# An attention and gated-MLP block on one core: a new order for background sums, more staging rows, norm transposes by DMA, and merged half tiles

## The chip, the cores and the metric

The kernel runs on one core of one Trainium2 chip. The metric is the device time in microseconds of one execution. Before the change it was 876.59 us (median of three runs, 875.39 to 877.72). The kernel before had medians of 873.2 to 876.6 us in different sessions, 0.4% apart, so each experiment is compared with the runs of the kernel before of its own session, on the same chip.

## The reference

One transformer block with 2,048 tokens of width 640, 32 heads of width 20, and a gated MLP of width 1,728, all in bf16:

```python
x = A_x                                    # 1 x 2048 x 640
h = x + attention(layernorm(x), wqkv, wo)  # softmax(q k^T / sqrt(20)) v, 32 heads
n = layernorm(h)
out = h + ((n @ w_gate) * (n @ w_up)) @ w_down
```

The score matrix is the large thing: 32 heads x 2,048 x 2,048 exps.

## The kernel before

The program is one static schedule. A small planner in Python keeps a model of the engines, picks at each step what TensorE (PE) does next, and so fixes the order of every engine's instructions. The lines of all matmuls are one helper line, so in the profile the tile names tell them apart.

Queries come in six chunks of 512, 512, 384, 256, 256 and 128. For each chunk PE makes scores into PSUM tiles `A` (two tiles, of three and of two banks), ScalarE (ACT) takes the exp of a whole tile into `E`, and PE sums `E` with the values into the bank `acc`. Between these, PE does background sums: the projections of Q, K and V, and then the second stage of the chunk before (output projection `W`, LayerNorm, transposes, gate and up sums, down sums). All of these share only two PSUM banks, `m`, until attention has ended.

Some of the exps are made on VectorE (DVE) from integer arithmetic, to take load off ScalarE. Such a score bank goes into a free `m` bank if there is one. If there is none, and the tile `A` with three banks is next, its third bank is used instead; then ACT's instruction covers only two banks:

```python
ok = fr and self.flat < M_END                 # fr: the m banks that are free now
if ok or size == 3:
    mine = banks if ok else banks[:2]
    ...
    if pick is not None and ok:
        dbank = min(fr, key=lambda b: b.free.t)   # an m bank; ACT keeps its full tile
    elif pick is not None:
        third = Bank(A[u][:, 2, :])               # the third bank of A; ACT gets two
```

The choice of PE's next work (first number: the earliest time, then the rank; lower goes first):

```python
opts.append((max(ep, t), 0, pact))                # value sums
opts.append((max(eb, t), 1, self.bg_act(g)))      # background sums
opts.append((es, 2, sact))                        # scores
```

Heads beyond the first eight have their Q and K projected densely, 120 rows at a time, and unpacked through DRAM. DVE moves the finished sum from its `m` bank into one of two staging rows, a DMA writes that out, another reads it back in the wanted layout:

```python
stg = tiles(p1, 2, [P, QW], BF16, "stg")
...
r = en.add("DVE", dve_ns(w), [e, stg_free[k]], ... copy of ps into stg[k] ...)
e = dma(write, [r], size=TW * w * 2)
stg_free[k] = e                                   # free when the DMA has landed
```

The norm of the second stage is transposed by PE, 20 column-tiled matmuls against the identity for each 128 x 640 tile, and copied from PSUM by DVE into `ln2T`. The MLP width of 1,728 is 13 tiles of 128 and one of 64; gate and up are two sums of five steps for each.

The softmax here doesn't subtract the row's maximum and nothing guards it: scores larger than these inputs give would overflow.

## Time and profile before

| | before |
|---|---|
| median | 876.59 us |
| profiled span | 873.6 us |
| first exp starts | 17.0 us |
| exps on ACT, busy | 800.0 us in 749 instructions, 1,746 banks |
| ACT pauses between exps | 20.5 us |
| last exp to the end | 36.1 us |
| exps on DVE | 302 banks, 176 from `m` and 126 from `A` |

The four rows from the first exp on (17.0, 800.0, 20.5 and 36.1) add to the span; that sum is how I read this kernel throughout. "Pauses" is worked out: end of the last exp, less start of the first, less busy time. Busy tenths in 40 equal slices of the span, which show that PE, DVE and ACT are all full in the middle, and that ACT has little to do in the last two slices:

```profile
PE   6999999989999999999999999999999999999998
...
DVE  5654587989879999999989999989999999889562
ACT  4789999999999999999999999999999999998931
```

The other two rows that matter are the second half of the DVE exps, and the copies after the PE transposes (count, then busy us and mean ns, then idle time before):

```profile
L745 DVE TENSOR_SCALAR i<-A 128x512 int16<-128x512 f32 x126 | 86.5, 686 | 11.5 <-PE A L432 10.0
...
L1026 DVE COPY ln2T<-m 128x640 bf16<-128x640 bf16 x15 | 7.2, 483 | 0.2 <-PE m L1017 0.2
```

### The profile page before, as it was taken

To read this page: it belongs to the slowest core of one execution; us is meant where nothing else is said; L and a number is where in the kernel's file an instruction comes from. 1 tells how busy PE (TensorE), PEld (TensorE's weight loads), DVE (VectorE), ACT (ScalarE), POOL (GpSimd) and SP (SyncE) were. 2 spreads that over 40 slices of the span, in tenths; PEclk is the share of its full clock that TensorE was granted. 3 is DMA by queue.
4 is the path that set the end of the run, shared out by engine and by line. 5 is a ranking of instruction groups with operands and counts; after the bars stand their busy time and mean duration, and the time that the engine had idled before them with its cause. 6 is when DMAs were issued, how large, how long until landed. Compare 5 with 4: busy or idle time off the path is not lost.

```text
span 873.6 us, 35178 instructions
## 1 busy us (share of the span) xinstructions
PE 828.6 (95%) x15727; PEld 366.7 (42%) x15727; DVE 741.9 (85%) x1579; ACT 808.8 (93%) x771; POOL 21.3 (2%) x33
## 2 busy tenths in 40 slices
PE   6999999989999999999999999999999999999998
PEld 3344333223333322233444333344444444556676
DVE  5654587989879999999989999989999999889562
ACT  4789999999999999999999999999999999998931
POOL 3020000000000000000000000000000000000000
PEclk8899999999999999999999999999999999999999
DMA  7221221222221143320030223134024411164200
GB/s 209 64 58 49 79 67 31 78 76 67 69 79 29 28 105 103 78 63 18 30 91 13 57 66 81 27 84 105 17 51 94 96 32 32 32 150 86 52 6 24
DMA packets 131755, 56.23 MB, mean 64 GB/s; under 512 B 102292, under 2 KB 129556, under 8 KB 131604
## 3 DMA queue, kind: packets, MB, share of 16 engines
q1 hardware_dynamic: 131604, 53.99, 24.3%
q8 instruction: 123, 2.02, 1.0%
q14 instruction: 28, 0.23, 0.1%
HBM read 45.63 MB, written 8.09 MB: 61 GB/s over the span
## 4 chain that ended last, share of the span: by engine, by line
ACT 63%; PE 26%; DVE 6%; issue 5%; DMA 0%; DVEq 0%; POOL 0%; ACTq 0%
ACT E L731 62%; PE m L432 11%; PE A L432 6%; PE acc L432 5%; PE b L432 2%; DVE i L745 2%; DVE fr L775 1%; PE m L1017 1%; DVE ED L778 1%; DVE st L989 0%; DVE fr L769 0%; DVE hl L772 0%; DVE gs L1410 0%; DMA shared<-in_A_x_dram 0%; DVE shared L1001 0%
## 5 line engine op out<-in xcount | busy, mean ns | idle before, releaser
L731 ACT ACTIVATE E<-A 128x1536 bf16<-128x1536 f32 (+1 forms) x749 | 800.0, 1211 | 20.6 <-PE A L432 18.4
L432 PE MATMUL A<-qT,kT 32*128 32x256 bf16 (+3 forms) x3063 | 292.7, 298 | 24.1 <-ACT E L731 21.9
L432 PEld LDWEIGHTS <-kT 32*128 32x128 bf16 (+1 forms) x3448 | 100.1, 92 | 248.2 <-issue 215.0
L432 PE MATMUL acc<-E,Vx 128*32 128x256 bf16 (+3 forms) x2832 | 190.7, 304 | 4.8 <-ACT E L731 3.8
L745 DVE TENSOR_SCALAR i<-m 128x512 int16<-128x512 f32 x176 | 120.4, 685 | 13.5 <-PE m L432 12.5
L432 PEld LDWEIGHTS <-Vx 128*32 128x32 bf16 x3328 | 70.1, 95 | 100.5 <-issue 91.6
L775 DVE TENSOR_TENSOR fr<-hl,fr 128x1024 bf16<-128x1024 bf16 x151 | 103.4, 685 | 2.0
L778 DVE TENSOR_TENSOR ED<-i,fr 128x1024 int16<-128x1024 int16 x151 | 103.0, 682 | 1.3
L745 DVE TENSOR_SCALAR i<-A 128x512 int16<-128x512 f32 x126 | 86.5, 686 | 11.5 <-PE A L432 10.0
L432 PE MATMUL m<-Wd,hh 128*32 128x320 bf16 (+1 forms) x1498 | 79.9, 301 | 1.4 <-issue 0.9
L432 PE MATMUL m<-lnT,Wr 128*32 128x512 bf16 (+7 forms) x1200 | 74.7, 345 | 1.8 <-DVE lnT L1026 0.8
L432 PE MATMUL m<-ln2T,wu 128*32 128x512 bf16 (+2 forms) x980 | 69.5, 348 | 0.8 <-DVE i L745 0.4
L432 PE MATMUL m<-ln2T,wg 128*32 128x512 bf16 (+2 forms) x980 | 69.2, 349 | 0.3 <-DVE hh L1421 0.2
L432 PE MATMUL acc<-zt 128*32 128x512 bf16 (+3 forms) x1012 | 68.5, 346 | 0.0
L432 PE MATMUL m<-qT,kT 32*128 32x256 bf16 (+3 forms) x265 | 68.0, 310 | 0.0
L772 DVE TENSOR_SCALAR hl<-fr 128x1024 bf16<-128x1024 int16 x151 | 63.5, 421 | 1.5
L769 DVE TENSOR_SCALAR fr<-i 128x1024 int16<-128x1024 int16 x151 | 62.1, 417 | 0.7
L432 PEld LDWEIGHTS <-hh 128*32 128x32 bf16 (+2 forms) x1540 | 42.2, 96 | 28.1 <-issue 15.5
L1421 DVE TENSOR_TENSOR hh<-gs,m 128x512 bf16<-128x512 bf16 (+3 forms) x70 | 37.9, 541 | 14.0 <-PE m L432 10.1
L432 PE MATMUL m<-shared,On 128*32 128x320 bf16 x960 | 44.7, 300 | 0.7 <-DVE i L745 0.4
L432 PEld LDWEIGHTS <-Wr 128*32 128x32 bf16 (+1 forms) x1200 | 28.9, 97 | 27.0 <-issue 16.7
L1410 DVE CAST gs<-m 128x512 bf16<-128x512 f32 (+2 forms) x64 | 36.0, 562 | 4.7 <-PE m L432 4.3
(85 smaller groups left out, 542.7 us busy)
## 6 DMA issues: line engine op xcount, KB each, us to landing
wg<-in_B_w_gate_dram SPq DMA_DIRECT2D x47, 160.0 KB
wu<-in_B_w_up_dram SPq DMA_DIRECT2D x47, 160.0 KB
rb<-rd SPq DMA_DIRECT2D x16, 256.0 KB
kT<-kq SPq DMA_DIRECT2D x24, 128.0 KB
kq<-stg SPq DMA_DIRECT2D x24, 120.0 KB
out_dram<-ot SPq DMA_DIRECT2D x16, 160.0 KB
shared<-in_A_x_dram SPq DMA_DIRECT2D x14, 160.0 KB
Wd<-in_B_w_down_dram SPq DMA_DIRECT2D x13, 160.0 KB
```

Source lines behind the costliest of these rows:

```text
L432: nc.tensor.matmul(out_, lhsT=lhsT, rhs=rhs, start=start, stop=stop)
L731: apart(readers, nc.scalar.activation(E[:, 0:size, :], src[:, 0:size, :], ACT.Exp, scale=LN2_ / UNIT))
L745: apart(readers, nc.vector.tensor_scalar(it[:, pos, :], bank.ap, BIAS, 0.0, ALU.add, ALU.max))
L769: nc.vector.tensor_scalar(f[:, 0:n, :], it[:, 0:n, :], 127, None, ALU.bitwise_and)
L772: nc.vector.tensor_scalar(h[:, 0:n, :], f[:, 0:n, :], QR, QK, ALU.subtract, ALU.mult)
L775: nc.vector.tensor_tensor(fb[:, 0:n, :], h[:, 0:n, :], f[:, 0:n, :], ALU.mult)
L778: nc.vector.tensor_tensor(e16[:, 0:n, :], it[:, 0:n, :], fb[:, 0:n, :], ALU.add)
L1017: nc.tensor.transpose(pt[32 * i:32 * i + 32, c * P:(c + 1) * P], src[:, c * P + 32 * i:c * P + 32 * i + 32], ident[:])
L1410: r = en.add("DVE", dve_ns(w), [e, was], lambda: nc.vector.tensor_copy(gs[0:M, 0:w], ps[0:M, 0:w]), 1)
L1421: r = en.add("DVE", dve_ns(w), [e, ce, was], lambda: nc.vector.tensor_tensor(hh[0:M, 0:w], gs[0:M, 0:w], ps[0:M, 0:w], ALU.mult), 1)
```

## The change

There are four parts.

**Order**: a background sum that already has a bank goes ahead of value sums, while no more than 14 exp'd banks wait for their value sum. **Rows**: five staging rows in place of two; they lie inside `ln2T`, which nothing else uses that early. **DMA turn**: in the first four chunks the norm tiles are transposed by a DMA. **Halves**: the half gate and up tiles lie side by side in one 128-wide weight tile and are summed at once.

```diff
+BACK = 14
-            opts.append((max(eb, t), 1, self.bg_act(g)))
+            opts.append((max(eb, t), 1 if g.bank is None or len(self.att.E) > BACK else -1, self.bg_act(g)))
...
-    stg = tiles(p1, 2, [P, QW], BF16, "stg")
+    stg = [ln2T[:, i, :] for i in range(KC)]
...
+TURNP = 4
+    def turn_rows(src, dst, deps, prio):
+        return dma(lambda: nc.sync.dma_start_transpose(dst, src), deps, prio=prio, size=2 * P * D * 2)
...
+                if p < TURNP:
+                    lev[i] = turn_rows(l2[i % 2][:], ln2T[:, :, i * P:(i + 1) * P], [e, fr.get("ln2T")], 0.5)
+                    fr["ln", i % 2] = lev[i]
+                    continue
...
+                if M < P:
+                    ...   # ev_gu: cast ps[0:M] to gs[M:2M], then hh = gs[M:2M] * ps[M:2M]
+                    gg = sum_group(..., [(wg[:, c, :], ln2T[:, c, 0:w]) for c in range(KC)], w, P, ev_gu, f"g{p}{f}")
```

Left out of this diff are the weight loads that put both halves into one tile.

More of the change, by code (lines that the diff above doesn't have):

```diff
@@ L1296, in hold @@
         w_ = tile_ap.rearrange("p (c f) -> p c f", c=KC)
-        e = dma(lambda: nc.sync.dma_start(w_[:, :, 0:M], src), deps, size=n, prio=3)
+        at = M if which == 1 and M < P else 0
+        e = dma(lambda: nc.sync.dma_start(w_[:, :, at:at + M], src), deps, size=n, prio=3)
         p2["held"][which, f] = (w_, e)
@@ L1322, in prefetch @@
         for n in range(2 * (NF - RES)):
-            ap, e = spots[n]
+            ap, e = spots[min(n, 2 * (NF - RES) - 2)]
             hold(n % 2, RES + n // 2, ap, [e])
@@ L1399, in more @@
                     src, _, n = weight(1, f)
-                    eu = dma(lambda wu=wu, src=src, M=M: nc.sync.dma_start(wu[:, :, 0:M], src), [fr.get(("wu", k))], prio=2, size=n)
+                    if M < P:
+                        eu = dma(lambda wg=wg, src=src, M=M: nc.sync.dma_start(wg[:, :, M:2 * M], src), [fr.get(("wg", k))], prio=2, size=n)
+                    else:
+                        eu = dma(lambda wu=wu, src=src, M=M: nc.sync.dma_start(wu[:, :, 0:M], src), [fr.get(("wu", k))], prio=2, size=n)
                 gk = gsn[0] % 2
@@ L1403, in more, with ev_gu @@
                 gs = T["gs"][gk]
+                if M < P:
+                    cu = Cell()
+                    def ev_gu(ps, e, gs=gs, M=M, cu=cu, hh=T["hh"][f], was=fr.get(("gs", gk)), then=fr.get(("hh", f))):
+                        cast = lambda: (nc.scalar.copy if last else nc.vector.tensor_copy)(gs[M:2 * M, 0:w], ps[0:M, 0:w])
+                        r = en.add("ACT", w / 1.2 + 63.0, [e, was], cast, 1) if last else en.add("DVE", dve_ns(w), [e, was], cast, 1)
+                        cu.t2 = en.add("DVE", dve_ns(w), [r, then], lambda: nc.vector.tensor_tensor(
+                            hh[0:M, 0:w], gs[M:2 * M, 0:w], ps[M:2 * M, 0:w], ALU.mult), 1)
+                        return cu.t2
+                    fr["gs", gk] = cu
+                    gg = sum_group(list(lev.values()) + [eg, eu, fr.get(("hh", f))], [(wg[:, c, :], ln2T[:, c, 0:w]) for c in range(KC)], w, P, ev_gu, f"g{p}{f}")
+                    if not held:
+                        fr["wg", k] = gg.ev
+                    groups.append(gg)
+                    hhev.append(cu)
+                    ups.append(gg.ev)
+                    continue
                 ce = Cell()
```

## The prediction

> **What bounds the kernel now.** I read the page first: busy times, then the chain that ended last. After that the waits, then windows of the busy times by stage, and last the timeline of the two ends. The page:
>
> ```profile
> span 873.6 us, 35178 instructions
> PE 828.6 (95%) x15727; PEld 366.7 (42%) x15727; DVE 741.9 (85%) x1579; ACT 808.8 (93%) x771; POOL 21.3 (2%) x33
> ...
> ACT 63%; PE 26%; DVE 6%; issue 5%; DMA 0%; DVEq 0%; POOL 0%; ACTq 0%
> ...
> L731 ACT ACTIVATE E<-A 128x1536 bf16<-128x1536 f32 (+1 forms) x749 | 800.0, 1211 | 20.6 <-PE A L432 18.4
> ...
> L745 DVE TENSOR_SCALAR i<-m 128x512 int16<-128x512 f32 x176 | 120.4, 685 | 13.5 <-PE m L432 12.5
> ...
> L432 PE MATMUL acc<-zt 128*32 128x512 bf16 (+3 forms) x1012 | 68.5, 346 | 0.0
> ```
>
> PE is the busiest by its share, but it does not bind: the last row above, `acc<-zt`, multiplies a tile of zeros, filler put where PE has nothing to do (76.5 us with its smaller groups, summed over windows of that tile). What binds is the exp on ScalarE (L731): 749 instructions, 800.0 us busy, 63% of the chain. Over time (columns: stretch, length, busy of PE, PEld, DVE, ACT, POOL with counts, clock, DMA share, GB/s):
>
> ```profile
> 60.00:140.00 80.00, 77.60 (x1406) 31.79 (x1402) 51.58 (x106) 77.53 (x71) 0.00 (x0) 1.00 0.22 65
> 140.00:300.00 160.00, 151.46 (x2298) 54.71 (x2290) 137.58 (x280) 159.46 (x155) 2.07 (x2) 1.00 0.21 60
> 300.00:740.00 440.00, 423.14 (x8011) 176.12 (x8009) 424.68 (x861) 435.50 (x407) 4.08 (x5) 1.00 0.26 62
> 740.00:838.00 98.00, 95.64 (x2772) 58.38 (x2768) 75.19 (x176) 93.38 (x91) 0.70 (x1) 1.00 0.34 74
> ```
>
> From 60 to 740 us ACT is 97 to nearly 100% busy. The span is therefore a sum of four terms: 17.0 us before the first exp (timeline), 800.0 us of exps, 20.5 us of ACT pauses among them, and 36.1 us from the last exp (837.5) to the end at 873.6. Where the pauses lie, from the waits (us in total, times, longest):
>
> ```profile
> ACT gs L1408 <- PE b L432: 27.4, 10, 20.3
> ACT E L731 <- PE A L432: 18.4, 17, 3.5
> ```
>
> The first is the tail, in which ACT only copies gate sums. Of the second, 8.6 us lie between 16 and 60 us, 2.4 from 60 to 120, 2.9 from 300 to 520 and 3.0 after 780. In the tail the timeline shows PE working almost without a gap (838 to 870 us): the rest of the fifth query chunk's gate and up sums, its down sums, then the same for the sixth. So the tail is bound by PE work left over when attention ends.
>
> VectorE matters because it takes exps off ScalarE. L745 with its four followers does 302 (176 from `m`, shown above, and 126 from `A`) of the 2,048 score banks (the scheduler's cap is 17%, about 320), ScalarE the other 1,746. One bank on DVE costs 0.685 us plus half of the four two-bank rows (0.417 + 0.421 + 0.685 + 0.682 = 2.205, so 1.10): 1.79 us. On ACT one costs 800.0 / 1,746 = 0.46 us. DVE is 97% busy from 300 to 740 (424.68 of 440), but idle 28 us in 60 to 140 and 22 us in 140 to 300.
>
> **What the Trainium skill says.** "VectorE: DVE Perf Modes", The three transpose paths, puts a 128x128 bf16 transpose at 390 ns on TensorE into PSUM and at 1,309 ns by DMA into SBUF. The trace of before has only the PE path: 20 column-tiled instructions for a whole 128x640 tile take 0.46 us together, far below five times the page's figure; no run yet shows the DMA. "DMA: Bandwidth & Descriptors", DMA Transpose (X-bar), says that two transposing streams in flight at once can corrupt each other; here all DMAs come from one queue, so no new wait should follow. "TensorE: Matmul & The Clock Gate", Part 4, says the PE's output goes to PSUM and needs a copy: agreed, there are 16 such copies into ln2T at 0.48 us each. "TensorEngine Tiling (Array Packing)", Key Properties, says that tiles of the array run independently: agreed, four column-tiled matmuls of 512 columns that each last some 390 ns come out in a group of 0.39 us, so a 64-wide tile fills half of the array in the same time.
>
> **The change part by part.**
>
> Norm transposes by DMA, in the first four chunks (4 + 4 + 3 + 2 = 13 of 16 row tiles). Removed: 13 x 20 transposes, 13 x 0.46 = 6.0 us of PE, and 13 copies, 13 x 0.483 = 6.3 us of DVE (row L1026), and 13 holdings of one of the only two `m` banks. Added: 13 DMAs of 160 KB. My estimate for one: five blocks at the skill's 1.31 us are 6.5 us if nothing overlaps, about 3 us if it moves like other transfers (held weights of 160 KB ran at 222 GB/s near 785 us, 0.7 us each, plus receipt). The scheduler plans for 0.73 of issue, 2.05 of transfer and 3.5 of landing, 6.3 us. The DMA queues carry 24.3% of their capacity. The PE share is hidden wherever filler runs. The DVE share is not: 6.3 / 1.79 is 3.5 exps moved, 3.5 x 0.46 = **1.6 us less on ACT**.
>
> Half gate and up tile in one sum. The last tile is 64 wide. Two sums of five become one of five; the cast and the product on DVE stay. Saved PE: five steps over all the columns of each chunk. A sum of five over 128 columns starts every 0.28 us in the tail (timeline), 0.44 ns a column and step, so 5 x 2,048 x 0.44 = 4.5 us. Only what lies after about 640 us, where background work runs over into the tail, is worth time: chunks of 384, 256, 256 and 128 columns, 5 x 1,024 x 0.44 = 2.2 us. The transposes of the third and fourth chunks add 5 x 0.46 = 2.3 us. Filler after 640 us still takes about 7 us, so part of it is hidden. I take two thirds of 4.5: **3 us off the tail**.
>
> Five staging rows. The dense K/Q projections stage in two rows that are freed only when a DMA has landed; meanwhile the finished sum sits in an `m` bank. They run from 71 to 300 us, the stretch in which DVE has 50 us idle and the share lies below its cap: counting L745, 79 banks by 300 us, where 17% of some 555 allows 94. If the freed banks give half of these 15, that is 7 exps, 7 x 0.46 = **3 us**. (The rows now lie inside ln2T, whose first transpose came at 290 us, while the last staging was at 299; the first DMA transposes may have to wait, which costs nothing as gate sums begin at 311.)
>
> Opened background sums ahead of value sums. No work is added or removed, only order: a sum that has a bank ends sooner, its bank frees sooner, K and Q come sooner. It applies while at most 14 exp'd banks wait. It can help the pauses before 120 us (8.6 + 2.4 = 11); most of these follow a LayerNorm-transposes-projection chain, in which only part is PE order. I take **1 us**.
>
> Against it: a pause where a gate sum waits for a late transpose. Before, a PE transpose and copy needed about 1.5 us. Four stages, **+0.6 us** in all.
>
> Sum: -1.6 - 3 - 3 - 1 + 0.6 = -8.0 us, 876.6 - 8.0 = 868.6 us, a ratio of 0.991.
>
> **The rivals.** (a) The new transposes come late and PE, which takes its instructions in order, stops with scores queued behind a gate sum. For it: one engine queue, and a skill figure (6.5 us) as long as the planned 6.3. Against: slack of 2 us is in the plan, gate sums are spread over the chunk, the queues are three quarters idle. If each of four stages lost 4 us, ACT would lose most of it, having only one or two exps queued: +14 us, about 883.
> (b) Nothing binding is removed. ACT keeps its 1,746 banks because the exps on DVE are held by other things (their four ED buffers, the two banks), and PE time saved turns into filler. For it: filler is 76.5 us already. Then only the tail moves: 873 to 874.
> (c) Value sums come later, E buffers stay full and ACT waits for them. For it: ACT has 3 + 5 buffers. Against: the 14-bank limit, with 19 banks of room. Some 2 to 4 us slower than my sum.
> (d) More than I took: the DVE share reaches its cap of about 320 (18 exps, 8 us), the tail gives 4 and the early pauses 4: 876.6 - 16 = 860.
>
> **Range and chances.** (a) in full I give 5%, (b) 25%, (d) in full 10%, the rest lies around the sum. Range 860.0 to 877.5. Faster by over 2% would need less than 859.1 us: even (d) falls just short, so 9%. Slower by over 2% needs 894.1, twice (a): 3%. Within 2%: 88%.
>
> **What would show it.** In the profile after: `ln2T<-m` copies fall from 15 to about 2; the PE transposes of `l` from 300 to about 40; DVE exps rise from 302 to some 308 to 318 and ACT's L731 falls from 800 to about 795. ACT still leads the chain with over 60%. The stretch from the last exp to the end shrinks from 36 to about 33 us. Wrong would be: a new wait of PE for the transpose DMA above 2 us in total, L731 busy unchanged, pauses before 120 us longer than 11 us, or a tail no shorter. The prediction fails most likely because a static schedule reacts to small changes as a whole: each part here shifts all that follows.

## The result, and the profile after

The changed kernel took 865.5 us (median of four runs, 864.96 to 867.77) against 875.99 us of the kernel before over its four runs. The ratio is 0.9887 with a 95% interval of 0.9857 to 0.9916. Predicted were 868.6 us and 0.991; the result is within the range, and within 2% of before.

The page of the changed kernel, with the lines that answer those of before:

```profile
span 863.1 us, 34690 instructions
PE 813.7 (94%) x15473; PEld 359.8 (42%) x15473; DVE 752.6 (87%) x1604; ACT 803.4 (93%) x751; POOL 20.6 (2%) x33
...
ACT 56%; PE 31%; DVE 8%; issue 5%; POOL 0%; DMA 0%; ACTq 0%; DVEq 0%; POOLq 0%
...
L734 ACT ACTIVATE E<-A 128x1536 bf16<-128x1536 f32 (+1 forms) x729 | 794.6, 1226 | 14.9 <-PE A L435 12.3
...
L748 DVE TENSOR_SCALAR i<-m 128x512 int16<-128x512 f32 x225 | 153.0, 683 | 14.5 <-PE m L435 13.3
...
L435 PE MATMUL acc<-zt 128*32 128x512 bf16 (+2 forms) x1008 | 66.7, 342 | 0.0
L748 DVE TENSOR_SCALAR i<-A 128x512 int16<-128x512 f32 x87 | 59.4, 683 | 6.4 <-PE A L435 5.4
```

PE lost 14.9 us of busy time and 254 matmuls, DVE gained 10.7 us, and ACT's exps went from 800.0 us in 749 instructions to 794.6 in 729. DVE makes 312 exps in place of 302. The larger shift is in where they come from: 225 from the `m` banks in place of 176, and 87 from `A` in place of 126. The same stretches of the span as in the prediction:

```profile
60.00:140.00 80.00, 77.46 (x1426) 32.83 (x1428) 58.61 (x120) 77.39 (x69) 0.00 (x0) 1.00 0.22 65
140.00:300.00 160.00, 148.63 (x2259) 54.26 (x2252) 154.98 (x317) 159.96 (x147) 1.43 (x2) 1.00 0.29 77
300.00:740.00 440.00, 421.87 (x7980) 172.57 (x7976) 416.76 (x841) 438.61 (x405) 3.84 (x5) 1.00 0.26 60
740.00:838.00 98.00, 94.95 (x2633) 62.57 (x2633) 75.66 (x192) 83.89 (x82) 1.35 (x2) 1.00 0.33 71
```

DVE, the third busy column, went from 51.58 to 58.61 us in the first and from 137.58 to 154.98 in the second: its idle time from 60 to 300 us fell from 51 to 26 us. (The last line reaches past the end of the exps in this kernel, so its ACT column isn't comparable.) The waits of ACT (us in total, times, longest):

```profile
ACT gs L1443 <- PE m L435: 24.3, 6, 20.9
...
ACT E L734 <- PE A L435: 12.3, 10, 4.7
```

The same sum for both kernels:

| | before | after | difference | predicted |
|---|---|---|---|---|
| to the first exp | 17.0 | 17.1 | +0.1 | 0 |
| exps on ACT, busy | 800.0 | 794.6 | -5.4 | -4.6 |
| ACT pauses | 20.5 | 14.7 | -5.8 | -0.4 |
| last exp to end | 36.1 | 36.6 | +0.5 | -3 |
| span | 873.6 | 863.1 | -10.5 | -8.0 |

So the total was nearly right, but of the terms that were to change only one was: pauses gave far more than I thought and the tail nothing. That the sum came near is partly luck, since a miss of -5.4 us on the pauses met one of +3.5 us on the tail. The experiments ask which of the four parts did this.

### The profile page after: what moved, and what is told of

It reads as the page before. It is cut to its first block, busy times and chain, and to the rows that moved or that the text cites. A ratio compares the mean times of both kernels' runs of the same rounds, so it can differ in the third digit from the quotient of the medians.

```text
span 863.1 us, 34690 instructions
## 1 busy us (share of the span) xinstructions
PE 813.7 (94%) x15473; PEld 359.8 (42%) x15473; DVE 752.6 (87%) x1604; ACT 803.4 (93%) x751; POOL 20.6 (2%) x33
## 4 chain that ended last, share of the span: by engine, by line
ACT 56%; PE 31%; DVE 8%; issue 5%; POOL 0%; DMA 0%; ACTq 0%; DVEq 0%; POOLq 0%
ACT E L734 55%; PE m L435 15%; PE A L435 8%; PE acc L435 6%; PE b L435 2%; DVE i L748 2%; DVE ED L781 1%; DVE fr L778 1%; DVE st L992 1%; PE m L1020 0%; DVE hl L775 0%; DVE hh L1456 0%; DVE fr L772 0%; DVE shared L1004 0%; DVE shared L1362 0%
## 5 line engine op out<-in xcount | busy, mean ns | idle before, releaser
L734 ACT ACTIVATE E<-A 128x1536 bf16<-128x1536 f32 (+1 forms) x729 | 794.6, 1226 | 14.9 <-PE A L435 12.3
L748 DVE TENSOR_SCALAR i<-m 128x512 int16<-128x512 f32 x225 | 153.0, 683 | 14.5 <-PE m L435 13.3
L778 DVE TENSOR_TENSOR fr<-hl,fr 128x1024 bf16<-128x1024 bf16 (+1 forms) x158 | 106.9, 676 | 1.9
L781 DVE TENSOR_TENSOR ED<-i,fr 128x1024 int16<-128x1024 int16 (+1 forms) x158 | 106.6, 675 | 1.5
L435 PE MATMUL m<-qT,kT 32*128 32x256 bf16 (+2 forms) x327 | 86.7, 315 | 0.0
L435 PE MATMUL m<-lnT,Wr 128*32 128x512 bf16 (+6 forms) x1200 | 73.8, 346 | 1.6 <-DVE lnT L1029 0.8
L775 DVE TENSOR_SCALAR hl<-fr 128x1024 bf16<-128x1024 int16 (+1 forms) x158 | 65.5, 415 | 1.9
L435 PE MATMUL acc<-zt 128*32 128x512 bf16 (+2 forms) x1008 | 66.7, 342 | 0.0
L772 DVE TENSOR_SCALAR fr<-i 128x1024 int16<-128x1024 int16 (+1 forms) x158 | 63.9, 411 | 0.6
L435 PE MATMUL m<-shared,On 128*32 128x320 bf16 (+1 forms) x968 | 46.5, 301 | 0.0
L435 PEld LDWEIGHTS <-zt 128*32 128x32 bf16 x1148 | 28.7, 97 | 24.6 <-issue 13.7
```

The lines of the kernel that those rows point to most:

```text
L435: nc.tensor.matmul(out_, lhsT=lhsT, rhs=rhs, start=start, stop=stop)
L734: apart(readers, nc.scalar.activation(E[:, 0:size, :], src[:, 0:size, :], ACT.Exp, scale=LN2_ / UNIT))
L748: apart(readers, nc.vector.tensor_scalar(it[:, pos, :], bank.ap, BIAS, 0.0, ALU.add, ALU.max))
L772: nc.vector.tensor_scalar(f[:, 0:n, :], it[:, 0:n, :], 127, None, ALU.bitwise_and)
L775: nc.vector.tensor_scalar(h[:, 0:n, :], f[:, 0:n, :], QR, QK, ALU.subtract, ALU.mult)
L778: nc.vector.tensor_tensor(fb[:, 0:n, :], h[:, 0:n, :], f[:, 0:n, :], ALU.mult)
```

## The experiments

**Theory M**: the gain comes from the turnover of the two `m` banks. A sum that is finished sooner, and moved out sooner, frees its bank for DVE exps. Then order and rows carry it. **Theory L**: the gain comes from the PE and DVE work that is taken away. Then DMA turn and halves carry it. A third reading, **chance**, is that a static schedule shifts with any edit and happened to fall well.

The numbers of exps and instructions in the expectations are counted in the built programs; no time in them is from a model of the chip. A DVE exp saves ACT about 0.43 us, and an ACT instruction less saves about 0.06 us. I had first taken these from the shape of the instructions. A fit over the fourteen profiles then gave 0.43 us for each bank and 0.062 us for each instruction, with no profile off by more than 1.4 us. The split is soft: a fit that also allows a constant divides the same saving into 0.22 and 0.15 us. The number of instructions follows from the exps that go into `m` banks: it is (2,048 - those) / 2.5 to within one in all fourteen profiles, as all other banks pass through the tiles `A` of three and of two banks.

The first expectations were written from 876 us. The kernel before took 873.2 us on the chip where they were tested, so the ratios decide, and not whether a time falls into a range.

### Each part alone

Order only, rows only, DMA turn only, halves only, each as its hunk of the diff above put on the kernel before. For the first:

```diff
-            opts.append((max(eb, t), 1, self.bg_act(g)))
+            opts.append((max(eb, t), 1 if g.bank is None or len(self.att.E) > BACK else -1, self.bg_act(g)))
```

> The kernel before with only the new order (opened background sums ahead of value sums while at most 14 exp'd banks wait). Theory M (the gain comes from how fast the two m banks turn over): this alone gives part of it. The built program has 303 DVE exps in place of 302 and 744 ACT exp instructions in place of 749, so ACT loses 0.43 + 0.3 = 0.7 us; if the ACT pauses (20.5 us) also shrink, by up to 5 us in all. So 870 to 875 us. Theory L (the gain comes from PE and DVE work that is taken away): nothing, 876.

Measured: 873.93 us against 873.23 on that chip, ratio 1.0007 (0.9992 to 1.0022). No gain.

```diff
-    stg = tiles(p1, 2, [P, QW], BF16, "stg")
+    stg = [ln2T[:, i, :] for i in range(KC)]
```

> The kernel before with only the five staging rows, inside ln2T (a separate place for five rows does not fit). The result may be wrong, since staging and the first transposes of the second stage may overlap there; time is what is asked. Theory M: the largest single part. 308 DVE exps in the built program, 743 ACT exp instructions: 6 x 0.43 + 6 x 0.06 = 3 us less ACT work, and fewer pauses: 869 to 873. Theory L: 876.

Measured: 878.00 us, ratio 1.0051 (1.0031 to 1.0070), and the result was correct. Half a per cent slower: my guess of the largest single part was wrong in sign.

```diff
+                if p < TURNP:
+                    lev[i] = turn_rows(...)
```

> The kernel before with only the 13 norm transposes by DMA. Theory L: 6 us of PE and 6.3 us of DVE less give 4 to 6 us, 871 to 873. Theory M: 304 DVE exps, same 749 ACT exp instructions: 0.9 us, 874 to 876.5; and if the DMA comes late, slower than before.

Measured: 877.51 us, ratio 1.0044 (1.0030 to 1.0057). Slower, although no wait for a transpose DMA appears among the waits; the time is in the stretch after the last exp, 42.0 us in place of 36.1.

```diff
+                if M < P:
+                    gg = sum_group(..., [(wg[:, c, :], ln2T[:, c, 0:w]) for c in range(KC)], w, P, ev_gu, ...)
```

> The kernel before with only the half gate and up tiles in one sum. Theory L: 4.5 us less PE, half of it late enough to shorten the tail: 2 us, 874. Theory M: 300 DVE exps, 751 ACT exp instructions, so nothing or slightly slower: 876 to 877. The tail from the last exp (36.1 us in the profile before) should stay within 0.7 us of that.

Measured: 870.14 us, ratio 0.9960 (0.9946 to 0.9974). Faster, but neither theory's way: the tail is 36.1 us as before, ACT busy 800.6, and the pauses are 13.1 us in its profile against 20.5 in that of before. (That is 7.4 us for a gain of 3.1 us: the profile of before is from a slower session, see below the table of all profiles.)

The four single differences, +0.07, +0.51, +0.44 and -0.40%, add to +0.6%. The whole change gives -1.1%. So the parts do not add, and one of them alone is not the cause.

### The change without each part

Each of these takes one hunk out of the changed kernel; in the third it is `TURNP = 0`.

```diff
-            opts.append((max(eb, t), 1 if g.bank is None or len(self.att.E) > BACK else -1, self.bg_act(g)))
+            opts.append((max(eb, t), 1, self.bg_act(g)))
```

> The changed kernel without the new order. Theory M (turnover of the two m banks): 310 DVE exps against 312 and 737 ACT exp instructions against 729 in the built program: 0.9 + 0.5 = 1.4 us more ACT work, and some pauses come back: 867 to 870. Theory L (work taken away): as the changed kernel, 865.5.

Measured: 875.78 us against 873.44, ratio 1.0015 (0.9992 to 1.0038). The whole gain is gone, which is more than theory M expected (867 to 870).

```diff
-    stg = [ln2T[:, i, :] for i in range(KC)]
+    stg = tiles(p1, 2, [P, QW], BF16, "stg")
```

> The changed kernel with two staging rows of their own in place of five. Theory M: 305 DVE exps, 745 ACT exp instructions: 3 + 1 = 4 us more ACT work and pauses back: 869 to 873. Theory L: 865.5 to 866.

Measured: 873.35 us, ratio 1.0006 (0.9993 to 1.0019). The whole gain is gone here too.

```diff
-TURNP = 4
+TURNP = 0
```

> The changed kernel with all norm transposes back on PE. Theory L: 6 us of PE and 6.3 of DVE come back: 869 to 871. Theory M: 312 DVE exps, 731 ACT exp instructions: 865 to 867.

Measured: 864.74 us, ratio 0.9903 (0.9890 to 0.9916). The gain is all there without the DMA transposes.

```diff
-                if M < P:
-                    ...
```

> The changed kernel with separate sums for the half gate and up tiles. Theory L: 4.5 us of PE come back, 2 us late: 867.5. Theory M: 313 DVE exps, 729 ACT exp instructions: 865 to 866.5; tail longer by at most 0.8 us.

Measured: 865.11 us, ratio 0.9905 (0.9892 to 0.9917). It is all there without the merged halves.

So order and rows are each necessary, and DMA turn and halves are each unnecessary. Theory L falls.

### Order and rows together

Both of the unnecessary parts out at once:

```diff
-TURNP = 4
+TURNP = 0
-                if M < P:
-                    ...
```

> The kernel before with the new order and the five rows together, without the DMA transposes and the merged halves. Theory M (turnover of the two m banks, for which both parts are needed): 309 DVE exps and 730 ACT exp instructions in the built program, against 302 and 749 before and 312 and 729 in the changed kernel; 1.3 us more ACT work than the changed kernel, so 865 to 868, ratio to before 0.99. Theory L (work taken away matters, or each part only shifts the schedule by chance): the parts alone gave +0.6 and +4.5 us, so 874 to 879.

Measured: 864.94 us against 873.54, ratio 0.9903 (0.9886 to 0.9921). Two parts that gain nothing alone give the whole gain together. The rows of ACT's exps and of DVE's exps from `m`, first with order only:

```profile
L732 ACT ACTIVATE E<-A 128x1536 bf16<-128x1536 f32 (+1 forms) x744 | 798.1, 1218 | 20.9 <-PE A L433 17.5
...
L746 DVE TENSOR_SCALAR i<-m 128x512 int16<-128x512 f32 x188 | 128.4, 684 | 22.0 <-PE m L433 20.8
```

With rows only:

```profile
L731 ACT ACTIVATE E<-A 128x1536 bf16<-128x1536 f32 (+1 forms) x743 | 797.9, 1205 | 29.2 <-PE A L432 26.3
...
L745 DVE TENSOR_SCALAR i<-m 128x512 int16<-128x512 f32 x190 | 129.2, 684 | 23.3 <-PE m L432 22.6
```

With both:

```profile
L734 ACT ACTIVATE E<-A 128x1536 bf16<-128x1536 f32 (+1 forms) x730 | 795.7, 1226 | 16.6 <-PE A L435 14.0
...
L748 DVE TENSOR_SCALAR i<-m 128x512 int16<-128x512 f32 x224 | 152.8, 685 | 16.8 <-PE m L435 15.4
```

Read the count ahead of the bar: 188 and 190 exps from `m` with one part, 224 with both, from 176. One part gives 12 or 14 more, both together 48. But this is not the interplay that the times show. In ACT's busy time the parts simply add: 1.9 us less with order, 2.1 with rows, 4.3 with both. What does not add is the pauses: 20.8 us with order, 29.1 with rows, 16.5 with both, from 20.5.

What each part does to the `m` banks can be seen in the staging copies. Order only, from the tile's own list (durations in ns, then the start of the first and of the last, in us):

```profile
L1204 DVE TENSOR_SCALAR stg<-m x24: 223/482/692, 44.7 to 300.5; 120x512 bf16<-120x512 f32 x8, 120x256 bf16<-120x256 f32 x8, 120x384 bf16<-120x384 f32 x4, 120x128 bf16<-120x128 f32 x4
```

Rows only, and then the changed kernel:

```profile
L1203 DVE TENSOR_SCALAR ln2T<-m x24: 277/482/692, 68.7 to 245.5; 120x512 bf16<-120x512 f32 x8, 120x256 bf16<-120x256 f32 x8, 120x384 bf16<-120x384 f32 x4, 120x128 bf16<-120x128 f32 x4
```

```profile
L1210 DVE TENSOR_SCALAR ln2T<-m x24: 277/478/691, 44.8 to 240.5; 120x512 bf16<-120x512 f32 x8, 120x256 bf16<-120x256 f32 x8, 120x384 bf16<-120x384 f32 x4, 120x128 bf16<-120x128 f32 x4
```

The order brings the first staging forward from 69 us to 45 (before the change it was 70.8), and the rows bring the last forward from 300 us to 241 to 246. With order alone the copies come in pairs, one for each row. The four of 384 columns, from the timeline of DVE (start, busy us):

```profile
214.30 1.01 DVE L1204 TENSOR_SCALAR stg<-m 120x384 bf16<-120x384 f32 x2
```

```profile
225.75 1.01 DVE L1204 TENSOR_SCALAR stg<-m 120x384 bf16<-120x384 f32 x2
```

and in the changed kernel:

```profile
205.97 0.55 DVE L1210 TENSOR_SCALAR ln2T<-m 120x384 bf16<-120x384 f32 x1
208.05 0.55 DVE L1210 TENSOR_SCALAR ln2T<-m 120x384 bf16<-120x384 f32 x1
210.91 0.55 DVE L1210 TENSOR_SCALAR ln2T<-m 120x384 bf16<-120x384 f32 x1
212.57 0.54 DVE L1210 TENSOR_SCALAR ln2T<-m 120x384 bf16<-120x384 f32 x1
```

There are 11.5 us from one pair to the next, while the changed kernel makes all four in 7.1 us. How long each finished sum sat in its bank is in the traces too. A dense sum is five steps, each with one tile of 24 columns (`128*24` in the profile), so the end of the fifth can be matched with the start of its staging copy, for all 40 sums (us, worked out from the instructions; the last two columns are counts of DVE exps that started before 300 us):

| run | finished sums wait for their copy | bank held, first step to end of copy | from `m` | from `m` + `A` |
|---|---|---|---|---|
| before | 91.1 | 188.7 | 40 | 79 |
| order only | 107.3 | 197.7 | 51 | 85 |
| rows only | 28.6 | 124.2 | 60 | 88 |
| order and rows | 26.4 | 119.3 | 77 | 96 |
| changed | 26.3 | 119.1 | 83 | 98 |
| changed, three rows | 52.4 | 142.2 | 77 | 93 |

So the rows alone take nearly all of the waiting away. With order alone the sums take less time (67.5 us in place of 74.5 from first to last step, all added) but wait longer for a row. In this stretch the exps from `m` nearly add, 11 and 20 more against 37 with both; the rest of the 48 comes after 300 us, when no staging is left. So theory M holds for one half of the gain: the rows speed the turnover of `m`, and both parts bring more exps there, which is the ACT term. It does not explain why each part alone gains no time: that lies in the pauses.

### How much is chance, and how many rows

The planner's number for the issue time of a DMA, changed by 5 ns, in both kernels. It adds and removes no work.

```diff
-ISSUE = 730.0
+ISSUE = 735.0
```

> The kernel before with one number of the planner's DMA model changed, from 730 to 735 ns of issue time. No work is added or removed; only the order of instructions shifts. It measures how far the time moves by chance of the schedule. If schedules are stable: 873 to 874.5, as before on this chip. If chance is large: anywhere from 869 to 878.

Measured: 876.05 us against 873.54, ratio 1.0028 (1.0014 to 1.0043). So an edit that means nothing moves this kernel by 0.3%.

> The changed kernel with the same nudge (730 to 735 ns in the planner's DMA model). 312 DVE exps, 731 ACT exp instructions. Stable: 865 to 866.5. Chance large: 861 to 870; if it falls at 870 or above, the gain of the change is mostly a lucky schedule.

Measured: 865.27 us, ratio 0.9906 (0.9886 to 0.9927). The gain outlives the nudge. The single results of +0.51, +0.44 and -0.40% are only little larger than the nudge of 0.28%, and I draw nothing from their signs.

```diff
-    stg = [ln2T[:, i, :] for i in range(KC)]
+    stg = [ln2T[:, i, :] for i in range(3)]
```

> The changed kernel with three staging rows in place of five. Theory M: what matters is that a finished sum does not wait for a row; the built program already has 312 DVE exps and 729 ACT exp instructions with three: 864 to 867. If five rows are needed: 868 to 872, toward the kernel with two (873.4).

Measured: 868.96 us against 873.54, ratio 0.9952 (0.9938 to 0.9967). Half of the gain. The counts are those of five rows: 226 exps from `m`, and 794.4 us of ACT exps. What differs is the pauses, 21.7 us in place of 14.7. So three rows already give the ACT term, and the pause term stands apart from it. (The profiled run, at 872.14 us, was the slowest of six and 3.2 us above their median, so 21.7 is more than is typical.)

All profiles as one table (us; pauses worked out as above):

| run | ACT exps | instructions | DVE exps from m + A | pauses | last exp to end |
|---|---|---|---|---|---|
| before | 800.0 | 749 | 176 + 126 | 20.5 | 36.1 |
| before, nudged | 799.3 | 749 | 176 + 126 | 19.1 | 36.6 |
| order only | 798.1 | 744 | 188 + 116 | 20.8 | 35.3 |
| rows only | 797.9 | 743 | 190 + 119 | 29.1 | 35.2 |
| DMA turn only | 798.8 | 749 | 177 + 128 | 17.5 | 42.0 |
| halves only | 800.6 | 751 | 172 + 129 | 13.1 | 36.1 |
| without order | 796.8 | 737 | 205 + 106 | 23.1 | 37.7 |
| without rows | 797.1 | 745 | 186 + 122 | 23.6 | 31.8 |
| without DMA turn | 795.0 | 731 | 220 + 92 | 15.3 | 34.2 |
| without halves | 793.5 | 729 | 226 + 87 | 13.2 | 39.4 |
| order and rows | 795.7 | 730 | 224 + 85 | 16.5 | 34.7 |
| changed, three rows | 794.4 | 729 | 226 + 86 | 21.7 | 37.1 |
| changed, nudged | 794.4 | 731 | 222 + 90 | 17.8 | 34.1 |
| changed | 794.6 | 729 | 225 + 87 | 14.7 | 36.6 |

The profile of before is of a run of 875.66 us, about 2 us above its medians in the sessions of the experiments. Rows only and three rows were profiled 2.2 and 3.2 us above their own medians. I read no difference of the total pauses below some 3 us from this table.

Where the pauses lie says more than their sum. Between 300 and 520 us they are 0.2 to 0.6 us in the five profiles with order and all five rows, and 1.1 to 5.6 us in the nine others (3.3 before, 4.7 with three rows). After 780 us no such line can be drawn: 1.3 to 4.3 us in the five, 1.2 to 7.0 in the nine.

No run beat the changed kernel clear of the noise. Order and rows alone reach 0.9903 with far less new code, and its interval overlaps that of the whole change, 0.9887.

## Why the prediction was right or wrong, point by point

**What binds.** Right: ACT's exps are still the largest term of the span and the largest share of the chain, 56%. I had said over 60%.

**ACT's exp work, -1.6 - 3 = -4.6 us.** The size was right, -5.4, and half of the reasons. The sum has a term that I left out. An exp that moves from the third bank of `A` to an `m` bank lets ACT take all three banks in one instruction: 39 fewer such cases and ten more DVE exps make 20 fewer instructions, 20 x 0.062 = 1.2 us, beside 10 x 0.43 = 4.3 us (by the first fit above). The -1.6 from DVE work freed by the DMA transposes was not there: without them ACT's exps take 795.0 us against 794.6, and there are 312 exps on DVE in both. DVE was given back 6.3 us, and spent 5.3 us less overall (757.9 to 752.6), but not on exps.

**Five rows, -3 us.** The mechanism, a finished sum that holds an `m` bank, is what the trace shows: the waiting fell from 91.1 to 28.6 us with rows alone. I named the right stretch of the span, and the seven exps came exactly (302 to 309). They gave 2.1 us less ACT work. The step that failed is that I took the pauses to stay as they were: with rows alone they are 8.6 us longer in the profiled run, and the kernel is slower by 0.5%.

**Order, -1 us.** Here the prediction said "No work is added or removed, only order", which is so, and looked only at the pauses before 120 us. Those did not move: in the waits of ACT the time from 16 to 120 us was 11.0 us and is 10.5. What order did was to bring more exps into `m` (51 in place of 40 before 300 us) and, with the rows, to shorten the later pauses. Taking it out of the changed kernel costs the whole gain, 2.2 us of it in ACT work and 8.4 in pauses.

**The tail, -3 us.** This step failed. I took two thirds of the late PE work saved, 4.5 us, off the stretch after the last exp; it measured +0.5. The work did come out: PE lost 14.9 us. The fourth chunk's last down sum was added on DVE at 819.60 us before and at 812.63 after, 7.0 us sooner. But attention itself ended 11.1 us sooner (837.5 to 826.5), and background work that would have lain beside it was left for the end. I had priced the tail as if attention stayed where it was. The two lines:

```profile
819.60 0.49 DVE L1443 TENSOR_TENSOR ot<-m,h 128x320 bf16<-128x320 f32 x1 [0.89 <-PE m L432]
```

```profile
812.63 0.49 DVE L1478 TENSOR_TENSOR ot<-m,h 128x320 bf16<-128x320 f32 x1 [1.96 <-PE m L435]
```

Across all runs the tail lies between 31.8 and 42.0 us and follows no part clearly. What sets it in a given schedule stays open.

**Pauses, -1 + 0.6 us.** Mis-sized: -5.8. In the waits of ACT, 300 to 520 us fell from 3.1 to 0.2 and the time after 780 from 3.8 to 2.4. The one pause of 2.2 us at 467 us in the kernel before, while PE ran 64 instructions of the output projection in a row, is not in the changed kernel. The cause is not settled. The stretch from 300 to 520 us is shorter in every kernel with order and five rows, and so belongs to the change; why is not shown. An earlier second stage is a rival that I can't rule out or in: the last staging copy starts at 240.5 us in place of 299.1 and the first gate sum at 298.9 in place of 311.5. But with rows alone these are 245.5 and 301.9, and the pauses of that stretch are 5.6 us. With both parts and five rows the pauses were 13.2 to 17.8 us in five profiles, and 19.1 and 20.5 in the two of before. But three rows had 21.7 and halves alone, with the old order and rows, 13.1. Some of this term is the fall of the schedule, and some 2 us may be the session of the profile of before. Other values of `BACK` were not tried.

**Rival (a), late transposes.** Did not happen. PE, ACT and DVE show no wait for one of the 13 transposes. The queue's own record (durations in ns, minimum, median and maximum):

```profile
L1036 SPq DMA_TRANSPOSE ln2T<-l x13: 1199/1238/2240, 279.8 to 709.9; - x13
```

One of them was alone for a moment, and the windows of half a microsecond show its traffic (the last two columns are the DMA share and GB/s):

```profile
629.58 1.20 SPq L1036 DMA_TRANSPOSE ln2T<-l  x1
```

```profile
630.50:631.00 0.50, 0.50 (x19) 0.29 (x18) 0.50 (x3) 0.50 (x1) 0.00 (x0) 1.00 0.54 117
631.00:631.50 0.50, 0.50 (x15) 0.29 (x18) 0.50 (x2) 0.50 (x1) 0.00 (x0) 1.00 3.04 172
631.50:632.00 0.50, 0.50 (x20) 0.24 (x12) 0.50 (x1) 0.50 (x2) 0.00 (x0) 1.00 0.42 8
```

Issue began at 629.58, and about nine tenths of its bytes (0.5 us at 117 and 0.5 us at 172 GB/s are 145 of 164 KB) had moved by 631.5, about 2 us later; the lower of my two estimates, 3 us with the landing, was the better one. The first gate sum of that chunk began at 636.26.

**Rival (b), nothing binding is removed.** By the runs without them, true for two of the four parts, DMA turn and halves, as they stand in this kernel. **Rival (c)**, value sums late, is not seen in the changed kernel: ACT's pauses shrank. **Rival (d)**: the DVE exps reached 312, not the cap of about 320.

**Which signs of the prediction came.** The copies into `ln2T` fell from 15 to 2, PE transposes of `l` from 300 to 40, DVE exps rose to 312, and ACT fell to 794.6: all as said. The tail at 33 us was not.

## What to carry to other kernels

Where one scarce buffer is filled, drained and handed on by different engines, two changes to its traffic can be worth nothing singly and much together; test them as a pair before dropping either. When parts do not add, compare them term by term: here the work of the bound added up, and only the pauses did not. A saving beside the bound is worth the time only if the bound stays where it was: when the bound ends sooner, hidden work comes out at the end. And in a kernel with a static, planned order, nudge a number that means nothing first, and read no result below what that moves (here at least 0.3%, from one nudge of each kernel).

## What the Trainium skill lacked or had wrong

- "VectorE: DVE Perf Modes", The three transpose paths, gives 1,309 ns for one 128x128 bf16 block by DMA. Here a whole 128x640 tile, five blocks, had about nine tenths of its bytes moved 2 us after its issue began, so the figure is not to be multiplied by the number of blocks: that estimate was 6.5 us.
- "DMA: Bandwidth & Descriptors", DMA Transpose (X-bar), has no time that a transpose holds the issuing queue; elsewhere the page has only a count of cycles, for small tiles from HBM. Here it was 1.24 us in the median, against 0.33 and 0.72 us for the two kinds of staging writes on the same queue.
- "TensorE: Matmul & The Clock Gate", Part 4, gives 390 ns for a 128x128 transpose in isolation and about 275 ns in one kernel. Here one record of a transpose lasts 0.22 us, and 20 column-tiled ones for five blocks took 0.46 us together, 92 ns a block, as they overlap: the figure for one is not to be multiplied. All 13 tiles are then 6 us of PE, and with them back on PE the kernel was no slower (864.74 us).
- No page says how to read a DMA share above 1, which the profile shows in the half microsecond of a transpose (3.04), and without one too (1.05 from 784 to 787 us in the kernel before).
